# Attention that feeds a routed expert layer: where v is issued, where exp of q stands, and how the first weights are issued

## The chip, the cores and the metric

The kernel runs on one core of one Trainium2 chip. The metric is the device time of one execution in microseconds (us). Before the change it is 229.13 us, the median of three runs (229.08, 229.13, 229.18).

## The reference

There are two stages. The first is an attention without a score matrix; q, k and v have 8 batches, 8 heads, 576 positions and 64 features per head. The second sends each of the 4608 resulting rows of 512 numbers to one of 8 experts, chosen by a hash of its token id.

```python
def _attn_ref(q, k, v):
    q_s = np.exp(q - np.max(q, axis=-1, keepdims=True))
    q_s = q_s / (np.sum(q_s, axis=-1, keepdims=True) + 1e-09)
    k_s = np.exp(k - np.max(k, axis=2, keepdims=True))
    k_s = k_s / (np.sum(k_s, axis=2, keepdims=True) + 1e-09)
    kv = np.einsum('bhsd,bhse->bhde', k_s, v)
    return np.einsum('bhsd,bhde->bhse', q_s, kv)

def _moe_ref(x, token_ids, w1, w2):          # x: 4608 rows of 512
    expert_idx = token_ids * np.int64(2654435761) % np.int64(8)
    for e in range(8):
        mask = expert_idx == e
        out[mask] = np.maximum(x[mask] @ w1[e], 0.0) @ w2[e]
    return out
```

## The kernel before

**Order.** Every engine gets one stream of instructions, in the order in which the Python code emits them. `em.op` and `em.dma` add an instruction to a stream together with the semaphore waits that its buffers need (`R` read, `W` written, `P` written in part). An instruction that waits holds up everything behind it in its own stream. So the order of the calls in the loop over batches is, engine by engine, the order of the work.

**Loads.** `load(b, p)` lets SyncE issue q and k of batch b (L291) into one of two buffers each; q of batch b+2 can be issued when exp of q of batch b is done, k of batch b+2 when exp of k of batch b is done. `load_v(b, n)` lets GpSimd issue v (L304), with a conversion to bf16 on the way, into slot n of four. The expert weights are issued by GpSimd too: `weights1_half` (L668), `weights1` (L660), `weights2` (L674). The first expert's weights lie where q and k of the even batches were.

**One batch, b, with p = b % 2.** In the order of the calls:

- `exp_k(p)`: ScalarE takes exp of k (L518) into `ek`.
- `transpose_q(p)`: TensorE transposes `eq` (L525); VectorE and ScalarE copy the result to `qT` (L535, L537, L538).
- `one_hot(b)`: VectorE builds the matrices that put rows in the order of their experts (L592).
- `sort(1-p, 0, 3)`: TensorE sorts the first two of four column blocks of batch b-1 by expert (L601), ScalarE copies the result to `xs` (L608, two instructions); this copy is called an evacuation. `sort(1-p, 2, 0)`, the second one, does the other two blocks. It stands behind `kv` except in the last batch, where it stands ahead of it.
- `kv(p, n)`: TensorE multiplies exp of k with v (L550; "the matmul with v"), VectorE divides by the sums (L555, L559).
- `exp_q(1-p, 0)` and `exp_q(1-p, 1)`: ScalarE takes exp of q of batch b+1 (L514), in two instructions.
- `qsum(p)` and `attend(p, ...)`: TensorE (L569, L577), and VectorE scales the rows into `xn` (L573, L582).
- `segments(b-1)`: GpSimd copies 16 segments of `xs` of batch b-1, eight experts by two groups of rows, to their places in `xT` (L645). `segments` is a generator; each `next` emits one copy. `run(gen, n)` emits up to n copies, all 16 by default. The addresses come from registers that `load_segments` loads. In the last two batches a part of the copies is done by VectorE.

The v of batch b+2 is issued in batch b ahead of these copies for b = 1 to 4 (v2 already in batch 0); v7 is issued in batch 6. In batch 6 the first expert's first weights follow it (two halves by columns, each in two parts, four issues of L668), and the copies of batch 5 stand behind them.

**The expert stage.** When the last batch is sorted, TensorE runs both layers for eight experts in turn: `l1` (L683) with its rectifier on ScalarE or VectorE (L690, L692), then `layer2` (L708). GpSimd scatters the rows to the output (L724). The first two steps of `l1` are emitted ahead of the last batch's sort. Columns 0 to 511 of the first layer's weights wait for the first half of the weights, columns 512 to 1023 for the second.

Of the kernel before, what the change touches and what calls it, by code (L numbers as in the profile page):

```python
# [164 lines left out]
def fused_kernel(nc, q, k, v, moe_token_ids, moe_w1, moe_w2, out):  # L165
    B, H, S, DH = q.shape
    NTOK = moe_token_ids.shape[0]
    E, D, F = moe_w1.shape
# [109 lines left out]
    def dv(fn, R=(), W=(), P=()):  # L278
        em.op("dve", fn, R, W, P)

    def ac(fn, R=(), W=(), P=()):
        em.op("act", fn, R, W, P)
# [5 lines left out]
    b_q, b_k = [Buf(), Buf()], [Buf(), Buf()]  # L288

    def load_one(nm, dst, src, b, p, bb):  # L290
        em.dma("sync", nm % p, lambda e: e.dma_start(  # L291
            dst[p][:].rearrange("p h c d -> p h (c d)"),
            src[b].rearrange("(a h) (p c) d -> (h p) a (c d)", h=2, p=64)), W=[bb[p]])
# [8 lines left out]
    def load_v(b, n, R=()):  # L302
        o = 3 * (n % 2)
        em.dma("pool", "d_v%d" % n, lambda e: e.dma_start(  # L304
            vx[n // 2][:, o:o + 2, :, :, :].rearrange("p a j c d -> p (a j) (c d)"),
            v[b].rearrange("(a h) (p c) d -> (h p) a (c d)", h=2, p=64)), R=R, W=[b_vx[n]])
# [24 lines left out]
    for h in range(2):  # L331
        for a in range(2):
# [8 lines left out]
       R=[b_tok], P=[b_ei])  # L341
# [9 lines left out]
       R=[b_ef2, bc["iota8"]], W=[b_flg])  # L351
# [5 lines left out]
          R=[b_flg, bc["upper"], bc["ones"]], W=[bk[6], bk[7]])  # L357
# [13 lines left out]
       R=[b_pr], W=[b_pos])  # L371
# [137 lines left out]
    def load(b, p):  # L509
        load_one("d_q%d", qf, q, b, p, b_q)  # L510
        load_one("d_k%d", kf, k, b, p, b_k)

    def exp_q(p, j):
        ac(lambda e: e.activation(eq[p][:, j, :, :, :].rearrange("p c a d -> p a c d"),  # L514
                                  qf[p][:, j::2, :, :], ACTF.Exp), R=[b_q[p]], W=[b_eq[p][j]])

    def exp_k(p):
        ac(lambda e: e.activation(ek[p][:].rearrange("p j c a d -> p a (j c) d"),  # L518
                                  kf[p][:].rearrange("p (a j) c d -> p a (j c) d", a=2), ACTF.Exp),
           R=[b_k[p]], W=[b_ek[p]])  # L520
# [21 lines left out]
    def kv(p, n):  # L542
        o, one = (0, 2) if n % 2 == 0 else (2, 0)
        a0 = 1 - one // 2
        fns = []
        for j in range(2):
            for c in range(NC):
                for h2 in range(2):
                    r = slice(64 * h2, 64 * h2 + 64)
                    fns.append(lambda e, j=j, c=c, h2=h2, r=r: e.matmul(  # L550
                        PB[:, 6 + h2, 192 * j:192 * j + 192], ek[p][r, j, c, :, :].rearrange("p a d -> p (a d)"),
                        vx[n // 2][r, o:o + 3, j, c, :], start=(c == 0), stop=(c == NC - 1)))
        em.op("pe", fns, R=[b_ek[p], b_vx[n]], W=[bk[6], bk[7]])
        KV = PB[:, 6:8, 0:384].rearrange("p h (j a x) -> p j h a x", j=2, a=3)
        dv(lambda e: e.reciprocal(out=rk[p][:].rearrange("p (j h) -> p j h", h=2), in_=KV[:, :, :, one, 0]),  # L555
           R=[bk[6], bk[7]], W=[b_rk[p]])
        for a in range(2):
            r = slice(64 * a, 64 * a + 64)
            dv(lambda e, a=a, r=r: e.tensor_tensor(  # L559
                out=kvn[p][r, :, a, :].rearrange("p (j h) x -> p j h x", h=2), in0=KV[r, :, :, a0 + a, :],  # L560
                in1=rk[p][r, :].rearrange("p (j h) -> p j h", h=2).unsqueeze(3).to_broadcast([64, 2, 2, DH]),
                op=ALU.mult), R=[bk[6], bk[7], b_rk[p]], W=([b_kvn[p]] if a == 0 else ()),
               P=(() if a == 0 else [b_kvn[p]]))
# [24 lines left out]
    def one_hot(b):  # L588
        p = b % 2
        for t in range(T):  # L590
            g, i = t // TG, t % TG
            dv(lambda e, g=g, i=i: e.tensor_scalar(  # L592
                out=oneh[p][g][:, i, :], in0=col16[:, 0:GW[g]], scalar1=pos[:, 2 * b + g, i:i + 1],
                scalar2=None, op0=ALU.is_equal),
               R=[b_pos, bc["col16"]], W=([b_oh[p][g]] if i == 0 else ()), P=(() if i == 0 else [b_oh[p][g]]))
# [23 lines left out]
    def load_segments(b, key, half=None):  # L619

        def ld(e):
            k = (key, half, b % 2 if half is not None else 0)
            if k not in regs:
                regs[k] = [e.alloc_register("rg%s%d_%d" % (key, i, len(regs)))
                           for i in range(4 * E if half is None else 2 * E)]
            rs = regs[k]
            if half is None:
                e.load(rs, rgi[0:1, 2 * b:2 * b + 2, :].rearrange("p g x -> p (g x)"))
            else:
                for g in range(2):  # L630
                    e.load(rs[8 * g:8 * g + 8], rgi[0:1, 2 * b + g, 8 * half:8 * half + 8])
        em.raw(key, ld, R=[b_rg])

    def segments(b, key="pool", half=None):
        p = b % 2
        for g in range(2):
            for ee in range(E) if half is None else range(4 * half, 4 * half + 4):
                def seg(e, ee=ee, g=g):
                    if half is None:
                        rs, o = regs[key, None, 0], 2 * E * g + 8 * (ee // 4) + ee % 4  # L640
                    else:
                        rs, o = regs[key, half, p], 8 * g + ee % 4
                    so = e.snap(rs[o], min_val=0, max_val=GW[g])  # L643
                    do = e.snap(rs[o + 4], min_val=CAPS * ee, max_val=CAPS * ee + CAP)
                    return e.tensor_copy(out=xT[:, :, bass.ds(do, SEG[g])],  # L645
                                         in_=xs[p][:, :, XO[g]:XO[g] + GW[g] + SEG[g]][:, :, bass.ds(so, SEG[g])])
                em.op(key, seg, R=b_xs[p] + ([] if b < B - 2 else [b_x5[ee]]), W=[(b_x5 if b < B - 2 else b_x7)[ee]])
                yield
# [16 lines left out]
    def weights1_half(ee, s, hf, R=()):  # L665
        fs = slice(hf * F // 2, hf * F // 2 + F // 2)
        for a in range(2):
            em.dma("pool", "d_w1h%d" % hf, lambda e, a=a: e.dma_start(  # L668
                w1b[s][64 * a:64 * a + 64, :, fs], moe_w1[ee].rearrange("(a g p) f -> a p g f", a=2, g=4)[a, :, :, fs]), R=R,
                W=([b_w1[s][hf]] if a == 0 else ()), P=(() if a == 0 else [b_w1[s][hf]]))  # L670
# [59 lines left out]
    def run(gen, n=2 * E):  # L730
        for _ in range(n):
            if next(gen, 0) == 0:
                break
# [7 lines left out]
    for b in range(B):  # L741
        p = b % 2
        last = b == B - 1
        exp_k(p)
        transpose_q(p)
        one_hot(b)
        if b > 0:
            sort(1 - p, 0, 3)
        if last:
            sort(1 - p, 2, 0)  # L750
        if b + 2 < B:
            load(b + 2, p)
        kv(p, b % 4)
        if 0 < b < B - 1:
            sort(1 - p, 2, 0)
        if not last:
            exp_q(1 - p, 0)
            exp_q(1 - p, 1)
        qsum(p)
        if b == 0:  # L760
            load_v(2, 2)
        elif b < B - 3:
            load_v(b + 2, (b + 2) % 4)
        elif b == B - 2:
            load_v(B - 1, 3)
        if b == B - 2:
            for s, bs in enumerate(([b_q[0], b_k[0]], [b_q[1], b_k[1]])):
                b_w1[s], b_w2[s] = [Buf(*bs), Buf(*bs)], Buf(*bs)
            weights1_half(0, 0, 0)
            weights1_half(0, 0, 1)  # L770
            load_segments(b - 1, "pool")
            run(segments(b - 1))
        elif last:
            weights1(1, 1)
            weights2(0, 0)
            for x in (b - 1, b):
                load_segments(x, "pool", 1)
                load_segments(x, "dve", 0)
            run(segments(b - 1, "pool", 1))
        elif b > 0:  # L780
            load_segments(b - 1, "pool")
            run(segments(b - 1))
        attend(p, 0, 2, 3)
        attend(p, 2, 2, 6)
        attend(p, 4, 1, 5)
        if b == 0:
            segment_table()
            widths()
        if b == 1:
            overflow()  # L790
        if b == 2:
            load_widths()
# [121 lines left out]
    for b in range(B):  # L914
# [11 lines left out]
        for ch in range(4):  # L926
# [4 lines left out]
                R=b_xn[0] + [b_id], W=bk[u:u + 2])  # L931
            ac(lambda e, ch=ch, u=u: e.activation(xg[:, ch, :].rearrange("p (h x) -> p h x", h=2),
                                                  PB[:, u:u + 2, 0:H2], ACTF.Copy), R=bk[u:u + 2], W=[b_xg[ch]])
        for ee in range(E):
# [5 lines left out]
            for t in range(T):  # L940
                u = layer2(NW, t, 2)
                m = flg[:, 2 * b + t // TG, ee, t % TG:t % TG + 1]
                if ee == 0:
                    dv(lambda e, t=t, u=u, m=m: e.tensor_scalar(out=yg[:, t, :], in0=PB[:, u, :], scalar1=m,
                                                                scalar2=None, op0=ALU.mult),
                       R=[bk[u], b_flg], W=[b_yg[t]])
                else:
                    dv(lambda e, t=t, u=u, m=m: e.scalar_tensor_tensor(
                        out=yg[:, t, :], in0=PB[:, u, :], scalar=m, in1=yg[:, t, :], op0=ALU.mult, op1=ALU.add),
                       R=[bk[u], b_flg], W=[b_yg[t]])  # L950
# [39 lines left out]
```

## Time and profile before

| | |
|---|---|
| median of three runs | 229.13 us |
| the profiled execution: its time, its span | 230.2 us, 228.4 us |
| busy: TensorE, VectorE, ScalarE, GpSimd | 198.9, 116.1, 105.7, 121.6 us |
| mean granted TensorE clock | 0.992 |
| exp of k (L518) starts, batch 1 to 7 | 20.19, 31.44, 40.53, 51.23, 60.87, 69.01, 77.15 us |
| v issued by GpSimd (L304), batch 2 to 7 | 12.9, 28.47, 36.35, 43.42, 52.53, 73.16 us |
| last k: issued, landed | 63.07, 73.7 us |
| unbroken run of TensorE in the expert stage | from 91.91 us |

The span runs from the first to the last instruction of the profiled execution; all starts count from its beginning. The four lines on batches come from the timelines of the engines and from the DMA answers (issue and time to landing). The idle time in front of a group of instructions stands in square brackets, with what ended it.

### The profile page before, as it was taken

What the parts mean: (1) busy time and instruction counts of PE and PEld (TensorE: products, weight loads), DVE (VectorE), ACT (ScalarE), POOL (GpSimd) and SP (SyncE); (2) the same over time, 40 slices, a digit from 0 to 9 for tenths busy, and PEclk for the clock granted to TensorE, in tenths of its full rate; (3) what the DMA queues carried; (4) which work ended last, traced back from release to release, by engine and by line L of the source; (5) the groups of instructions that cost most, each with busy time, mean ns of one, the idle gap of its engine ahead of it and who ended that gap; (6) DMA issues with size and microseconds to landing.
All of it is one profiled execution on the core that took longest, in us unless ns stands there. A gap on an engine that the chain in (4) does not pass through costs nothing.

```text
span 228.4 us, 4640 instructions
## 1 busy us (share of the span) xinstructions
PE 198.9 (87%) x1786; PEld 134.5 (59%) x1788; DVE 116.1 (51%) x265; ACT 105.7 (46%) x133; POOL 121.6 (53%) x235
## 2 busy tenths in 40 slices
PE   0459968876899788999999999999999999999990
PEld 0348757654776564775574764754855845845640
DVE  1678798782778867699941322322421422412220
ACT  3385588756888944765342331331422322322311
POOL 8740778773659993670007975805715615125053
PEclk9999999997999999999999999999999999999999
DMA  6999999999996999799993799999999798113023
GB/s 208 295 371 293 292 372 316 301 312 351 297 401 250 149 196 195 119 153 204 207 177 139 160 204 205 330 272 201 290 200 242 163 203 224 73 46 139 24 102 123
DMA packets 29776, 50.25 MB, mean 220 GB/s; under 512 B 2351, under 2 KB 15663, under 8 KB 29744
## 3 DMA queue, kind: packets, MB, share of 16 engines
q0 software_dynamic: 20768, 30.94, 67.1%
q1 hardware_dynamic: 8976, 18.91, 22.9%
q8 instruction: 16, 0.26, 0.4%
q14 instruction: 16, 0.13, 0.2%
HBM read 61.90 MB, written 10.49 MB: 317 GB/s over the span
## 4 chain that ended last, share of the span: by engine, by line
PE 62%; DMA 20%; POOL 6%; ACT 5%; issue 4%; POOLq 1%; DVE 1%; SPq 1%; DVEq 0%; ACTq 0%
PE ps L708 29%; PE ps L683 27%; DMA kf<-in_k_dram 20%; POOL xT L645 4%; PE ps L601 3%; ACT ek L518 3%; PE ps L550 2%; ACT eq L514 1%; POOL out_dram L724 1%; ACT xs L608 1%; PE ps L819 1%; DVE xn L582 1%; POOLq L643 1%; POOL w1b L668 0%; POOL w1b L660 0%
## 5 line engine op out<-in xcount | busy, mean ns | idle before, releaser
L724 POOL DMA_INDIRECT out_dram<-yo,idx x40 | 39.5, 987 | 71.6 <-ACT yo L718 31.8
L708 PE MATMUL ps<-w2b,hT 128*128 128x512 bf16 x320 | 70.4, 379 | 0.0
L683 PE MATMUL ps<-xT,w1b 128*128 128x320 bf16 (+1 forms) x512 | 64.4, 286 | 0.8 <-ACT hT L690 0.8
L683 PEld LDWEIGHTS ps<-xT,w1b 128*128 128x128 bf16 x512 | 49.7, 98 | 15.1 <-ACT hT L690 1.1
L708 PEld LDWEIGHTS ps<-w2b,hT 128*128 128x128 bf16 x320 | 31.2, 98 | 36.3
L645 POOL COPY xT<-xs x112 | 39.6, 412 | 19.4 <-ACT xs L608 17.9
L690 ACT ACTIVATE hT<-ps 128x640 bf16<-128x640 f32 x41 | 28.8, 703 | 39.4 <-PE ps L683 39.0
L718 ACT ACTIVATE yo<-ps 128x512 f32<-128x512 f32 x26 | 15.5, 597 | 54.1 <-PE ps L708 54.1
L692 DVE TENSOR_SCALAR hT<-ps 128x640 bf16<-128x640 f32 x23 | 19.0, 825 | 30.2 <-PE ps L683 30.2
L720 DVE COPY yo<-ps 128x512 f32<-128x512 f32 x14 | 9.7, 692 | 44.0 <-PE ps L708 44.0
L601 PE MATMUL ps<-oneh,xn 128*128 128x384 bf16 (+1 forms) x160 | 25.0, 307 | 1.3 <-ACT qT L537 1.0
L582 DVE TENSOR_TENSOR xn<-ps,rq 128x1024 bf16<-128x1024 f32 (+1 forms) x24 | 23.6, 1041 | 3.2 <-PE ps L577 2.6
L608 ACT ACTIVATE xs<-ps 128x768 bf16<-128x768 f32 (+1 forms) x32 | 19.1, 651 | 9.2 <-PE ps L601 9.1
L518 ACT ACTIVATE ek<-kf 128x2304 bf16<-128x2304 f32 x8 | 17.0, 2123 | 9.9 <-DMA kf<-in_k_dram 9.9
L550 PE MATMUL ps<-vx,ek 64*128 64x192 bf16 x288 | 15.2, 264 | 7.2 <-ACT ek L518 7.2
L601 PEld LDWEIGHTS ps<-oneh,xn 128*128 128x128 bf16 x160 | 14.8, 102 | 10.1 <-issue 2.5
L514 ACT ACTIVATE eq<-qf 128x1152 bf16<-128x1152 f32 x16 | 17.7, 1162 | 2.0 <-DMA qf<-in_q_dram 2.0
L550 PEld LDWEIGHTS ps<-vx,ek 64*128 64x128 bf16 x288 | 12.9, 102 | 9.0 <-ACT ek L518 8.5
L525 PE MATMUL ps<-ident,eq 128*128 128x128 bf16 x144 | 12.2, 244 | 5.0 <-ACT eq L514 5.0
L525 PEld LDWEIGHTS ps<-ident,eq 128*128 128x128 bf16 x144 | 10.0, 111 | 6.1 <-ACT eq L514 5.7
L592 DVE TENSOR_SCALAR oneh<-col,pos 128x384 bf16<-128x384 f16 (+1 forms) x40 | 13.5, 403 | 0.0
L674 POOL DMA_DIRECT2D w2b<-in_moe_w_dram x16 | 12.4, 798 | 0.0
(101 smaller groups left out, 131.1 us busy)
## 6 DMA issues: line engine op xcount, KB each, us to landing
qf<-in_q_dram SPq DMA_DIRECT2D x8, 1152.0 KB, 15.7
kf<-in_k_dram SPq DMA_DIRECT2D x8, 1152.0 KB, 16.9
w2b<-in_moe_w_dram POOLq DMA_DIRECT2D x16, 512.0 KB, 11.5
w1b<-in_moe_w_dram POOLq DMA_DIRECT2D x14, 512.0 KB, 9.3
vx<-in_v_dram POOLq DMA_DIRECT2D x8, 576.0 KB, 11.1
w1b<-in_moe_w_dram POOLq DMA_DIRECT2D x4, 256.0 KB, 7.8
out_dram<-yo,idx POOLq DMA_INDIRECT x40, 4.4
tok<-in_moe_token_ids_dram SPq DMA_DIRECT2D x1, 36.0 KB, 5.6
```

The source lines that it names most:

```text
L514: ac(lambda e: e.activation(eq[p][:, j, :, :, :].rearrange("p c a d -> p a c d"), qf[p][:, j::2, :, :], ACTF.Exp), R=[b_q[p]], W=[b_eq[p][j]])
L518: ac(lambda e: e.activation(ek[p][:].rearrange("p j c a d -> p a (j c) d"), kf[p][:].rearrange("p (a j) c d -> p a (j c) d", a=2), ACTF.Ex ...
L525: return e.transpose(PBH[:, o:o + 128], eq[p][:, j, c, :, :].rearrange("p a d -> p (a d)"), ident[:])
L550: fns.append(lambda e, j=j, c=c, h2=h2, r=r: e.matmul(PB[:, 6 + h2, 192 * j:192 * j + 192], ek[p][r, j, c, :, :].rearrange("p a d -> p (a ...
L582: dv(lambda e: e.tensor_tensor(out=xn[p][:, t0:t0 + n, :].rearrange("p t (g x) -> p (t g) x", x=DH), in0=PB[:, bank:bank + n, :].rearrange ...
L601: em.op("pe", [lambda e, g=g, i=i, k=k, n=n: e.matmul(PB[:, bank + (k if g == 0 else 2), (0 if g == 0 else GW[1] * k):(GW[0] if g == 0 els ...
L608: ac(lambda e, g=g, src=src: e.activation(xs[p][:, c0:c0 + 2, XO[g]:XO[g] + GW[g]], src, ACTF.Copy), R=bs, P=b_xs[p][c0:c0 + 2])
L645: return e.tensor_copy(out=xT[:, :, bass.ds(do, SEG[g])], in_=xs[p][:, :, XO[g]:XO[g] + GW[g] + SEG[g]][:, :, bass.ds(so, SEG[g])])
L683: em.op("pe", [lambda e, d=d, k=k: e.matmul(cut(PB[:, u + k, 0:H2]), w1b[s][:, d, 128 * (f + k):128 * (f + k) + 128], cut(rhs(d)), start=( ...
L690: ac(lambda e: e.activation(o, i, ACTF.Relu), R=bk[u:u + 2], W=[b_hT[hp][hf][f // 2]])
L708: em.op("pe", [lambda e, fc=fc: e.matmul(PB[:, u, :], hT[hp][:, fc, 128 * t:128 * t + 128], w2b[s][:, fc, :], start=(fc == 0), stop=(fc == ...
L724: em.dma("pool", "d_o%d" % y, lambda e: e.indirect_dma_start(out=out[:, :], out_offset=IndirectOffsetOnAxis(ap=idx[:, 5 * ee + t:5 * ee + ...
```

## The change

Three things are moved, and nothing is added to the computation. First, in batches 0 to 6 the two exp instructions of the next q stand ahead of `kv` and of the second sort, so ScalarE does them before the second evacuation. Second, v2 is issued once k1 has landed; v4, v5, v6 and v7 are issued in batches 2, 3, 4 and 5, each behind the first of the 16 segment copies of that batch (v3 stays in batch 1, ahead of them). Third, in batch 6 the first half of the first weights is issued behind the first segment copy and the second half behind seven more, where both halves stood ahead of all the copies.

```diff
         if b + 2 < B:
             load(b + 2, p)
+        if not last:
+            exp_q(1 - p, 0)
+            exp_q(1 - p, 1)
         kv(p, b % 4)
         if 0 < b < B - 1:
             sort(1 - p, 2, 0)
-        if not last:
-            exp_q(1 - p, 0)
-            exp_q(1 - p, 1)
         qsum(p)
         if b == 0:
-            load_v(2, 2)
-        elif b < B - 3:
-            load_v(b + 2, (b + 2) % 4)
-        elif b == B - 2:
-            load_v(B - 1, 3)
+            load_v(2, 2, R=[b_k[1]])
+        elif b == 1:
+            load_v(3, 3)
         if b == B - 2:
             for s, bs in enumerate(([b_q[0], b_k[0]], [b_q[1], b_k[1]])):
                 b_w1[s], b_w2[s] = [Buf(*bs), Buf(*bs)], Buf(*bs)
+            load_segments(b - 1, "pool")
+            sg = segments(b - 1)
+            run(sg, 1)
             weights1_half(0, 0, 0)
+            run(sg, E - 1)
             weights1_half(0, 0, 1)
-            load_segments(b - 1, "pool")
-            run(segments(b - 1))
+            run(sg)
...
         elif b > 0:
             load_segments(b - 1, "pool")
-            run(segments(b - 1))
+            sg = segments(b - 1)
+            run(sg, 1)
+            if 1 < b < B - 2:
+                load_v(b + 2, (b + 2) % 4)
+            run(sg)
```

## The prediction

> **What bounds the kernel now.** I read the chain of waits first: from 92 us on it is TensorE alone (L683 and L708 in turn, no idle), so the expert stage ends a fixed time after the last batch's sort. In front of that, the timeline of ScalarE shows when each batch b may start: exp of k (L518, "ek b" below), then seven more instructions in order.
>
> ```profile
> 51.23 2.12 ACT L518 ACTIVATE ek<-kf 128x2304 bf16<-128x2304 f32 x1 [2.45 <-DMA kf<-in_k_dram]
> ...
> 57.69 1.19 ACT L608 ACTIVATE xs<-ps 128x768 bf16<-128x768 f32 x2 [2.35 <-PE ps L601]
> ...
> 60.87 2.12 ACT L518 ACTIVATE ek<-kf 128x2304 bf16<-128x2304 f32 x1
> ...
> 73.97 1.19 ACT L608 ACTIVATE xs<-ps 128x768 bf16<-128x768 f32 x2 [0.84 <-PE ps L601]
> 75.04 2.22 ACT L514 ACTIVATE eq<-qf 128x1152 bf16<-128x1152 f32 x2
> 77.15 2.12 ACT L518 ACTIVATE ek<-kf 128x2304 bf16<-128x2304 f32 x1
> ```
>
> ek 4 at 51.23 waited for k4. After that ScalarE runs through: ek 5, 6, 7 start at 60.87, 69.01, 77.15, that is 8.14 us apart, with 0.84 us idle in each batch ahead of the second evacuation (L608). From ek 7 to the first matmul of the unbroken run (91.91) are 14.8 us that the change leaves in their order. So the time moves as ek 7 moves.
>
> The second view is the table of stretches (columns: PE, PEld, DVE, ACT, POOL busy, clock, DMA share, GB/s), the third the DMA answers for 58 to 60 us and for k7 and v7.
>
> ```profile
> 54.00:58.00 4.00, 4.00 (x39) 2.64 (x36) 1.03 (x3) 1.65 (x4) 0.00 (x0) 0.57 1.06 362
> 58.00:59.00 1.00, 1.00 (x33) 1.00 (x31) 0.39 (x1) 1.00 (x3) 0.00 (x0) 1.00 1.12 290
> 65.00:66.00 1.00, 1.00 (x11) 0.74 (x10) 0.81 (x2) 0.17 (x1) 0.00 (x0) 1.00 1.08 421
> 72.00:73.00 1.00, 1.00 (x24) 0.78 (x19) 0.51 (x3) 1.00 (x3) 1.00 (x5) 1.00 0.42 155
> ```
>
> ```profile
> q0 software_dynamic: 171, 0.20, 56.6%
> q1 hardware_dynamic: 171, 0.38, 55.3%
> ...
> vx<-in_v_dram POOLq DMA_DIRECT2D x1, 576.0 KB, 6.0
> ...
> kf<-in_k_dram SPq DMA_DIRECT2D x1, 1152.0 KB, 10.6
> ```
>
> The DMA engines are full from 3 to 72 us. q and k go in order through the hardware queue, v through the software queue. Alone, the first moves about 409 GB/s (64 to 66 us); beside a v it falls to 0.38 MB in 2 us, 190 GB/s, while v gets 98. A q or k (1.18 MB) is 2.88 us alone. A v (0.59 MB) flows for 6.0 us and costs the other queue 6.0 x (409-190)/409 = 3.2 us. k7, issued at 63.07, lands at 73.7, and v7 is issued only then:
>
> ```profile
> 52.53 0.74 POOL L304 DMA_DIRECT2D vx<-in_v_dram  x1
> 59.13 5.67 POOL L645 COPY xT<-xs  x16 [5.86 <-ACT xs L608]
> 67.56 5.66 POOL L645 COPY xT<-xs  x16 [2.75 <-ACT xs L608]
> 73.16 0.74 POOL L304 DMA_DIRECT2D vx<-in_v_dram  x1
> ```
>
> Last, TensorE: after 2.54 us without work its clock fell to 0.50 for 3.4 us (54.2 to 57.6), and ten matmuls of the sort took 2.55 instead of 1.47 us. At 79.3 it idled 0.98 us and stayed at 1.00.
>
> ```profile
> 53.40 2.21 PE L550 MATMUL ps<-vx,ek 64*128 64x192 bf16 x36 [2.54 <-ACT ek L518]
> 55.55 2.55 PE L601 MATMUL ps<-oneh,xn 128*128 128x384 bf16 x10
> ...
> 77.88 1.47 PE L601 MATMUL ps<-oneh,xn 128*128 128x384 bf16 x10
> 80.33 1.47 PE L601 MATMUL ps<-oneh,xn 128*128 128x384 bf16 x10 [0.98 <-ACT qT L537]
> ```
>
> **exp of q moved.** Two L514 (2.2 us together) go ahead of two L608; nothing is added. TensorE's transposes no longer wait for them (0.39 + 0.43 us a batch in the late ones). But the gain is not that: sort, matmul with k, second sort, attend, VectorE's scaling and the next sort follow one another, by the rows of batch 5 1.59 + 1.32 + 0.50 + 0.69 + 2.35 (two of three scalings) + 0.05 + 1.44 = 7.94 us against 8.14. So 0.2 us a batch where nothing is awaited. The price: the second evacuation, and the copies and v behind it on GpSimd, come up to 2.2 us later, and with them exp waits for q to land. SP issues each q about 2 us sooner, which changes no order in a queue that is never empty.
>
> **v2 waits for k1.** k1 lands at 20.19; v2's issue moves from 12.9 to 20.2. Behind it on GpSimd is L381, idle until 23.65 anyway: nothing. v1 flows until about 22.3, so v2 flows 24.3 to 30.3 and lands at 32.0, and the matmul needs it at 33.6: nothing, with 1.6 us in hand. v3 keeps its 28.47.
>
> **v4 to v7 behind a copy.** Issue = end of the second evacuation + 0.25 (as 58.88 to 59.13) + 0.35 for one copy. The bytes begin 4.05 us after the issue (28.47 to 32.5; 52.53 to 56.5), flow 6.0 us and are landed 1.75 us later (38.5 to 40.3). For q and k I run the two rates on from k3, whose bytes are through at 38.7 by the running sum of the queue; done for the kernel before, this gives ends that the landings follow by 2.1 us (alone) or 3.3 us (beside a v), and k7 at 71.4, landed 73.7. exp of q starts when q has landed, and 4.1 us behind ek at the earliest (60.87 to 64.99); the evacuation ends 1.1 us behind it, or 3.9 us behind the start of the matmul with v. Now the change, batch by batch.
>
> v4 is issued at 39.6 (evacuation after q3's exp, 35.6 to 37.8, ends at 39.0), flows 43.7 to 49.7, lands 51.4. q4 is through at 41.6, landed 43.7; k4: 2.1 us alone, then 0.32/0.19 = 1.7, through 45.4, landed 48.7, which is 2.5 us sooner than before. ek 4 at 48.7, but its matmul waits for v4: 51.4 (before 53.4).
>
> v5: exp of q4 44.6 to 46.8, evacuation to 47.9, issue 48.5, flows 52.6 to 58.6, lands 60.3. q5 through 50.6, landed 52.7; k5 54.6, landed 57.9. The matmul of batch 5 waits for v5: 60.3 (before 63.05).
>
> v6: exp of q5 52.9 to 55.1, evacuation to 56.2, issue 56.9, flows 60.9 to 66.9, lands 68.6. q6 through 59.6, landed 61.7; k6 64.4, landed 67.7. Matmul of batch 6 at 67.7 + 2.2 = 69.9 (before 71.19).
>
> v7: exp of q6 62.1 to 64.3, evacuation to 65.4, issue 66.0, bytes from 70.1. q7 is through at 68.6. k7: 1.5 us alone (0.61 MB), the rest beside v7, 0.57/0.19 = 3.0 us, through 73.1, landed 76.4. So v7 gives k7 a delay of 2.7 us, which the slack of 77.15-73.7 = 3.4 us nearly takes up.
>
> ScalarE would be free for ek 7 at 75.1 (exp of q7 71.8 to 74.0, then the evacuation). It waits for k7: 76.4. **The sum**: 76.4-77.15 = -0.75 us; span 228.4 to 227.65, profiled 230.2 to 229.45. The profiled time is 1.07 above the median, so the median goes to 229.13-0.75 = 228.4. The bounds of this term: v7 issued 1 us sooner puts k7 at 77.5 (+0.35), 1 us later at 75.2 (-1.95).
>
> Against this the page "DMA: Bandwidth & Descriptors" of the Trainium skill, section "Rules for kernel authors", says to issue a DMA early and wait late; its section "Anatomy of one DMA" gives 2.0 us plus bytes at 436 GB/s, by estimate 3.4 us for a v, whose 0.59 MB would delay k7 by 1.4 us, to 75.1, and the time would be 227.1. The trace has 11.3 us for v6 beside q and k, and I keep the row.
>
> **First weights in two issues.** The same four L668 (2.48 us) now stand behind one and behind eight copies. The evacuation ends at 75.1 as before (75.16), so the first half is issued at 75.8 and 76.4 instead of 73.9 and 74.5; with the 7.3 us that its second part took before it lands at 83.7, needed by the first L683 at 85.70-0.75 = 85.0. The second half, issued at 79.5 and 80.2, lands 8.9 us later at 89.1, needed at 91.2. Expert 1's weights follow when the copies are through, at 75.4 + 5.65 + 2.5 = 83.6 instead of 81.92; with 8.4 us (81.92 to the second landing, 90.3) they land at 92.0, needed two steps of 1.05 us behind 91.2, at 93.3. All are covered by 1.3 us; uncovered, they would cost what they are late. The copies themselves start up to 2.5 us sooner; nobody on the path waits for them.
>
> **The rivals.** (1) Slower: TensorE cools. While ek 7 waits for k7, the sort of batch 6 ends at 77.8 (69.9 + 7.94) and the next sort waits for the qT copy, 3.0 us behind ek 7, at 79.4: 1.6 us idle, against 0.98 now. The clock held at gaps of 1.05 us and fell at 2.54; between lies the point from which this decides. If it falls, 3.4 us at half speed hit that sort and the matmul with v: batch 0's matmul with v, cold, took 3.06 us for 1.66, the sort above 2.55 for 1.47. Half of 3.4 us, 1.7, is the most that is lost; with 1.6 the time is 230.0, slower than before. The page "TensorE: Matmul & The Clock Gate", Part 1, names an idle window of about 3.4 us; by that 1.6 us would cost nothing and the sum would stand; but the 2.54 us above did cost.
> (2) Faster: v7's bytes begin at 71 or later (a later matmul of batch 5), pass behind k7, and ScalarE sets ek 7 at 75.1 to 75.3: -1.95, 227.2.
> (3) v7 flows wholly ahead of k7's end: 73.7 + 3.2 = 76.9 up to 77.5, so 228.9 to 229.5, and the rest of the change brings nothing.
>
> **How the numbers follow.** Forecast 0.47, own range 227.6 to 229.2; rival 1 0.27; rival 2 0.14; rival 3 0.12. A run of this kernel can tell about 0.2%, 0.46 us. Faster by more (ek 7 before 76.7): 0.31 of the forecast's share and all of rival 2, 0.45. Within: 0.14 of the forecast and half of rival 3, 0.20. Slower: rival 1, the other half of rival 3 and 0.02 of the forecast, 0.35. The range takes in rival 2's end and rival 1 with 0.6 more: 227.2 to 230.6.
>
> **What would show it.** ek 4 near 48.7 with its matmul held until about 51.4, matmul of batch 5 near 60.3, no half clock at 54; v7 issued near 66; ek 7 idle ahead of it on kf, near 76.4. Wrong if ek 7 starts without waiting for k7, if the clock drops after 78 us, or if the first L683 waits for w1.

## The result, and the profile after

The changed kernel takes 229.25 us (median of 4 runs, 228.99 to 229.48), the kernel before 229.16 in the same comparison. The ratio is 1.0004 with a 95% interval of 0.9987 to 1.0021: no change that can be told. Measured again in a second comparison, it is 0.9997 (0.9980 to 1.0015). Ratios go by fast runs; the only slow one below, a run of e3 at 231.37 us, is left out of its ratio.

The profiles say something else at first sight: the span went from 228.4 to 227.2 us. The timeline of ScalarE in the changed kernel, with the idle time ahead of a group in brackets:

```profile
47.63 2.15 ACT L518 ACTIVATE ek<-kf 128x2304 bf16<-128x2304 f32 x1
...
58.10 2.12 ACT L518 ACTIVATE ek<-kf 128x2304 bf16<-128x2304 f32 x1 [1.86 <-DMA kf<-in_k_dram]
...
67.69 2.12 ACT L518 ACTIVATE ek<-kf 128x2304 bf16<-128x2304 f32 x1 [2.29 <-DMA kf<-in_k_dram]
...
73.79 1.20 ACT L608 ACTIVATE xs<-ps 128x768 bf16<-128x768 f32 x2
75.86 2.12 ACT L518 ACTIVATE ek<-kf 128x2304 bf16<-128x2304 f32 x1 [0.86 <-DMA kf<-in_k_dram]
```

Batch 4 starts 3.6 us sooner than the 51.23 of before. But batches 5, 6 and 7 now each wait for their k, which before they did not, and of the 3.6 us 1.29 are left at batch 7 (75.86 for 77.15). The unbroken run of TensorE starts at 90.62, 14.76 us behind, as before. GpSimd's timeline and the DMA answers show what the last k shares its way with:

```profile
65.95 0.46 POOL L645 COPY xT<-xs  x1 [2.96 <-ACT xs L608]
66.46 0.74 POOL L304 DMA_DIRECT2D vx<-in_v_dram  x1
```

```profile
vx<-in_v_dram POOLq DMA_DIRECT2D x1, 576.0 KB, 9.9
...
kf<-in_k_dram SPq DMA_DIRECT2D x1, 1152.0 KB, 15.5
```

v7, issued at 66.46, lands at 76.4; k7, issued at 60.29, lands at 75.8, where it landed at 73.7 before. In the table of stretches (PE, PEld, DVE, ACT, POOL busy, clock, DMA share, GB/s) the changed kernel has no half clock at 54 us; it has one from about 39.6 to 43 us. Its DMA engines are still full at 72 us, with v7 beside k7 (264 GB/s), when before they had largely run dry (0.42, 155 GB/s):

```profile
39.00:40.00 1.00, 0.46 (x5) 0.59 (x8) 1.00 (x2) 0.87 (x2) 0.00 (x0) 0.80 1.05 417
40.00:41.00 1.00, 1.00 (x13) 1.00 (x11) 1.00 (x3) 0.54 (x1) 0.81 (x2) 0.50 1.04 408
...
54.00:58.00 4.00, 3.96 (x68) 3.43 (x66) 3.04 (x6) 1.98 (x3) 2.00 (x5) 1.00 1.13 288
...
72.00:73.00 1.00, 1.00 (x17) 0.81 (x16) 0.63 (x2) 1.00 (x2) 0.46 (x2) 1.00 1.16 264
```

So there were two questions. Why do 1.2 us of span not appear in the time? And is v7 what holds the last k?

### The profile page after: what moved, and what is told of

Same layout as the page of the kernel before. It is cut to its first block, busy times and chain, and to the rows that moved or that the text cites. A ratio compares the mean times of both kernels' runs of the same rounds, so it can differ in the third digit from the quotient of the medians.

```text
span 227.2 us, 4641 instructions
## 1 busy us (share of the span) xinstructions
PE 197.4 (87%) x1786; PEld 134.2 (59%) x1788; DVE 122.4 (54%) x265; ACT 105.6 (46%) x133; POOL 122.2 (54%) x235
## 4 chain that ended last, share of the span: by engine, by line
PE 60%; DMA 24%; ACT 4%; issue 4%; DVE 3%; POOL 2%; DVEq 1%; SPq 1%; POOLq 0%; ACTq 0%
PE ps L708 28%; PE ps L683 27%; DMA kf<-in_k_dram 19%; DMA vx<-in_v_dram 5%; PE ps L601 3%; ACT ek L518 2%; POOL out_dram L724 2%; DVE xn L582 2%; PE ps L550 1%; DVEq L631 1%; ACT eq L514 1%; ACT qT L537 1%; SPq L291 1%; PE ps L824 1%; ACT xs L608 0%
## 5 line engine op out<-in xcount | busy, mean ns | idle before, releaser
L724 POOL DMA_INDIRECT out_dram<-yo,idx x40 | 39.6, 990 | 71.5 <-ACT yo L718 31.8
L683 PEld LDWEIGHTS ps<-xT,w1b 128*128 128x128 bf16 x512 | 49.8, 98 | 14.9 <-ACT hT L690 1.1
L518 ACT ACTIVATE ek<-kf 128x2304 bf16<-128x2304 f32 x8 | 17.0, 2127 | 13.4 <-DMA kf<-in_k_dram 13.4
L592 DVE TENSOR_SCALAR oneh<-col,pos 128x384 bf16<-128x384 f16 (+1 forms) x40 | 19.6, 556 | 0.0
L550 PE MATMUL ps<-vx,ek 64*128 64x192 bf16 x288 | 13.6, 246 | 6.6 <-ACT ek L518 5.0
L550 PEld LDWEIGHTS ps<-vx,ek 64*128 64x128 bf16 x288 | 11.7, 95 | 8.2 <-ACT ek L518 6.2
L577 PE MATMUL ps<-kvn,qT 128*128 128x128 bf16 x160 | 11.3, 231 | 2.1 <-DVE kvn L559 2.1
```

Source lines behind the costliest of these rows:

```text
L550: fns.append(lambda e, j=j, c=c, h2=h2, r=r: e.matmul(PB[:, 6 + h2, 192 * j:192 * j + 192], ek[p][r, j, c, :, :].rearrange("p a d -> p (a ...
L592: dv(lambda e, g=g, i=i: e.tensor_scalar(out=oneh[p][g][:, i, :], in0=col16[:, 0:GW[g]], scalar1=pos[:, 2 * b + g, i:i + 1], scalar2=None, ...
L683: em.op("pe", [lambda e, d=d, k=k: e.matmul(cut(PB[:, u + k, 0:H2]), w1b[s][:, d, 128 * (f + k):128 * (f + k) + 128], cut(rhs(d)), start=( ...
L724: em.dma("pool", "d_o%d" % y, lambda e: e.indirect_dma_start(out=out[:, :], out_offset=IndirectOffsetOnAxis(ap=idx[:, 5 * ee + t:5 * ee + ...
```

## The experiments

Theory A: the profiled execution of before was one of its longer ones, lengthened by the half clock at 54 us. Theory C: the toll is v7, whose bytes flow ahead of the last k. Their rivals (B, D, E and others) stand in the expectations. "Last exp of k" is the start of L518 of batch 7. Medians are of 9 to 12 runs (e12: one run); ratios are to the kernel before, run beside them.

| run | what it is | median us | ratio (95%) | last exp of k | last k landed |
|---|---|---|---|---|---|
| e1_before_again | before | 229.92 | 1.0003 (0.9980 to 1.0026) | 77.43 | 73.65 |
| e12_before_third | before, one run | 229.13 | - | 76.04 | 73.8 |
| e8_warm | before, gap filled | 229.46 | 0.9996 (0.9975 to 1.0016) | 75.92 | 73.7 |
| e2_after_again | changed | 229.47 | 0.9997 (0.9980 to 1.0015) | 75.85 | 75.8 |
| e3_expq_only | exp of q alone | 228.30 | 0.9937 (0.9914 to 0.9959) | 74.81 | 73.4 |
| e4_without_expq | changed, exp of q back | 229.66 | 1.0001 (0.9984 to 1.0019) | 76.54 | 76.5 |
| e5_k3_free | changed, k3 not held | 229.60 | 1.0005 (0.9984 to 1.0027) | 76.11 | 76.1 |
| e6_v7_late | changed, v7 late | 228.06 | 0.9928 (0.9903 to 0.9952) | 74.38 | 73.3 |
| e7_expq_v7 | exp of q, v7 early | 228.75 | 0.9987 (0.9952 to 1.0022) | 75.35 | 75.3 |
| e9_expq_weights | exp of q, weights | 228.16 | 0.9942 (0.9923 to 0.9962) | 75.03 | 73.7 |
| e10_v7_late_v2_early | e6, v2 at once | 228.31 | 0.9940 (0.9917 to 0.9963) | 75.10 | 73.8 |
| e11_v6_ahead | e10, v6 ahead of the copies | 228.44 | 0.9955 (0.9929 to 0.9982) | 75.07 | 73.7 |

**Which execution of before the profile showed.** e1_before_again and e12_before_third are the kernel before, unedited; e2_after_again is the changed one.

> The kernel before, unchanged, for a second profile and its spread. Theory A: the profiled execution shown so far was 1.07 us above its median because of the half clock at 54 to 58 us, which most executions don't have. Then a new profile has a span near 227.3 us, no half clock behind 50 us, batch 5's exp of k near 59.8 and the last one near 76.1 us instead of 77.15. Rival B: the half clock is regular; then the span is 228.4 again with the last exp of k at 77.15, and the 1.3 us that the change gained there in its profile are lost in its other executions.

> The changed kernel, unchanged, for a second profile. Theory A: span 227.1 to 227.7 us, last exp of k at 75.8 to 76.4 us behind a wait for the last k, expert stage as before (136.6 us from the unbroken run to the end); time as before within 0.2%. Rival B: the last exp of k again near 75.9 us, but a half clock behind 78 us or a longer stage behind it, 228.4 us of span.

> The kernel before, unchanged, one more profile. Theory A: of its executions some have the half clock at 54 us (near 230.5 us) and more have not (near 229.2 us). If this one lies below 229.8 us, it has no half clock between 50 and 58 us and its last exp of k starts near 75.9 to 76.3 us; if it lies above 230 us, it has it, and the last exp of k starts near 77.2. Rival: the two don't go together.

e1's profiled execution took 230.62 us and had the half clock again, from 53.6 to 57 us. Theory A had expected a profile without it, so after e1 rival B stood. Its other runs lie from 229.07 to 230.54. One more profile, e12, caught an execution of 229.13 us. Its stretches and ScalarE's timeline:

```profile
38.00:42.00 4.00, 2.51 (x32) 2.60 (x35) 3.66 (x6) 3.09 (x3) 4.00 (x11) 0.78 1.09 339
42.00:46.00 4.00, 4.00 (x55) 3.13 (x52) 2.58 (x8) 2.98 (x4) 2.24 (x7) 0.79 1.12 289
54.00:58.00 4.00, 4.00 (x80) 3.45 (x74) 1.81 (x5) 3.16 (x6) 1.39 (x4) 1.00 1.04 406
```

```profile
72.85 1.19 ACT L608 ACTIVATE xs<-ps 128x768 bf16<-128x768 f32 x2 [0.84 <-PE ps L601]
73.93 2.22 ACT L514 ACTIVATE eq<-qf 128x1152 bf16<-128x1152 f32 x2
76.04 2.12 ACT L518 ACTIVATE ek<-kf 128x2304 bf16<-128x2304 f32 x1
```

Here the half clock lies a batch earlier, from about 40 to 44 us, ahead of the wait for k4, which takes the loss up; TensorE then comes late to that wait and idles 0.80 us there instead of 2.54. The clock stays full at 54, and the last exp of k starts at 76.04. Three profiles of before thus go with theory A: 230.2 and 230.62 us with the drop at 54, 229.13 us without. e2 for its part repeats the changed kernel's profile: 75.85, behind a wait for k7, with the runs from 228.95 to 230.03.

**Filling the gap.** In the kernel before, with `warm()` new:

```diff
+        if b == 4:
+            warm()     # 28 matmuls of ident with ones into bank 6, which kv overwrites
         kv(p, b % 4)
```

> The kernel before with 28 matmuls of 128 columns on constants (about 1.8 us) in front of batch 4's matmul with v, in the gap in which TensorE waits for k4; their result is overwritten. Theory A (the kernel before has executions with a half clock at 54 us and executions without, about 1.2 us apart): no half clock near 54 us, batch 5's exp of k near 60 us, the last one near 76.0 to 76.3, no time above 229.8 us, median 229.1 to 229.4. Rival: the half clock is not what parts the executions; then times near 230.5 us remain, or the last exp of k stays at 77.2.

No run of 12 lies above 229.94 us, where 10 of the 34 runs of before beside it lie above 230.0. Batch 5 starts at 59.28 and the last exp of k at 75.92. So the upper times go with the half clock at 54 us: they are gone when TensorE has work in the gap. Two expectations were missed: two runs lie just above 229.8 us (229.82 and 229.94), and the median, 229.46, is not lower than that of before (229.42), against the 229.1 to 229.4 expected. Only the upper part of the spread went.

**One part of the change at a time.** e3 is the kernel before with only the exp moved; e4 is the changed kernel with only that move taken back:

```diff
 e3 (against before)                     e4 (against the changed kernel): the reverse
+        if not last:
+            exp_q(1 - p, 0)
+            exp_q(1 - p, 1)
         kv(p, b % 4)
         if 0 < b < B - 1:
             sort(1 - p, 2, 0)
-        if not last:
-            exp_q(1 - p, 0)
-            exp_q(1 - p, 1)
```

> Only exp of q moved; v and the weights as in the kernel before. Theory A: with v early and v7 late the last k lands near 73.7 us, so ScalarE and TensorE set the last exp of k: 0.2 us a batch over the last three, 0.6 us, near 75.5 us, time 0.5 to 0.7 us below before. Rival: the move gains nothing, because exp of q now waits for q to land in batches 1 to 4 and the second evacuation comes late; then the time is that of before within 0.2 us.

> The change without the move of exp of q: v and the first weights as changed, exp of q behind the second sort as before. Theory A: the last k lands near 76 to 77 us because v7 flows ahead of it, and the last exp of k waits for it: time 0 to 0.8 us above before. Rival: v costs nothing there, ScalarE's own order sets the last exp of k at 8.14 us a batch from an earlier batch 4; then the time is up to 1 us below before.

The move of exp of q alone is worth 0.63% (0.41% to 0.86%); the medians are 1.25 us apart (229.55 and 228.30), about twice the 0.5 to 0.7 us expected. In its profile k7 has landed at 73.4 and ScalarE comes to the last exp of k from its own work:

```profile
73.75 1.20 ACT L608 ACTIVATE xs<-ps 128x768 bf16<-128x768 f32 x2
74.81 2.15 ACT L518 ACTIVATE ek<-kf 128x2304 bf16<-128x2304 f32 x1
```

Without it the v's and the weights change nothing that can be told (1.0001), and the last exp of k stands at 76.54 behind k7. So the whole change is a gain of 0.6% that its other part takes back, though by itself that part costs nothing that can be told.

**Is it v7?** e6 is the changed kernel with v7 in batch 6 again; e7 is e3 with v7 alone in batch 5:

```diff
 e6, batches 2 to 5 and batch 6
-            if 1 < b < B - 2:
+            if 1 < b < B - 3:
                 load_v(b + 2, (b + 2) % 4)
...
+            load_v(B - 1, 3)
             load_segments(b - 1, "pool")
             sg = segments(b - 1)
 e7, against e3: the load_v(B - 1, 3) of batch 6 gone, and
-            run(segments(b - 1))
+            sg = segments(b - 1)
+            run(sg, 1)
+            if b == B - 3:
+                load_v(B - 1, 3)
+            run(sg)
```

> The changed kernel with v7 issued in batch 6 again, ahead of the copies; all else as changed. Theory C: the last k lands near 73.0 to 73.7 us, the last exp of k is set by ScalarE near 74.8 to 75.1, time 0.8 to 1.1 us below the changed kernel, about that of the kernel in which only exp of q moved. Rival D: the last exp of k stays at 75.5 or later and the time within 0.3 us of the changed kernel.

> Exp of q moved, and of the v's only v7, into batch 5 behind the first copy; v2 to v6 and the weights as in the kernel before. Theory C: this alone gives the toll: the last k lands 2 to 2.7 us later than with v7 late (73.42), near 75.5 to 76, the last exp of k waits for it, time 0.8 to 1.2 us above the kernel in which only exp of q moved. Rival D: the last exp of k stays near 74.8 and so does the time.

With v7 late (issued at 72.0) k7, issued at 60.23, lands at 73.3 instead of 75.8, and the last exp of k follows ScalarE's own work:

```profile
kf<-in_k_dram SPq DMA_DIRECT2D x1, 1152.0 KB, 13.1
```

```profile
73.30 1.19 ACT L608 ACTIVATE xs<-ps 128x768 bf16<-128x768 f32 x2 [0.62 <-PE ps L601]
74.38 2.12 ACT L518 ACTIVATE ek<-kf 128x2304 bf16<-128x2304 f32 x1
```

The kernel is 0.72% (0.48% to 0.97%) faster than before. Here the last exp of k no longer sets the expert stage. TensorE's own rows do, with both sorts of batch 6 in one piece:

```profile
70.52 1.66 PE L550 MATMUL ps<-vx,ek 64*128 64x192 bf16 x36 [0.84 <-DMA vx<-in_v_dram]
...
77.03 2.78 PE L601 MATMUL ps<-oneh,xn 128*128 128x384 bf16 x20 [0.82 <-DVE xn L582]
...
89.94 5.32 PE L683 MATMUL ps<-xT,w1b 128*128 128x320 bf16 x38
```

The sort waits for VectorE's scaling behind batch 6's matmul with v, which had waited for v6, and the unbroken run starts 15.56 us behind the last exp of k instead of 14.76. So the 0.43 us that this exp starts ahead of e3's (74.38 for 74.81) are not passed on: e3's unbroken run starts at 89.65.

e7 is the counter-test: v7 alone, issued at 67.7, lets k7 (issued at 61.11) land at 75.3, where it landed at 73.4 in e3:

```profile
kf<-in_k_dram SPq DMA_DIRECT2D x1, 1152.0 KB, 14.2
```

The last exp of k starts 0.54 us behind that of e3, less than the 0.8 to 1.2 us that the time was expected to rise. Only about 0.25 us of it are the wait for k7: ScalarE was free at 75.10 (1.06 us behind the start of the evacuation at 74.04, as in e3). The other 0.29 us were there in batch 6 (67.94 for 67.65), when v7 had only just been issued. v7 was also issued 1.2 us later than in the changed kernel, so e7 shows the delay of the last k, 1.9 us, but little of its price. Its ratio is too wide to say more: 3 of the 12 runs lie from 230.6 to 231.6 us, as does one of e3's ten (231.37), and what lengthened them stays open.

**A wait that I had missed.** The changed kernel's SyncE timeline:

```profile
18.24 0.37 SPq L291 DMA_DIRECT2D qf<-in_q_dram  x1
32.09 0.37 SPq L291 DMA_DIRECT2D kf<-in_k_dram  x1
```

k3 is issued at 32.09, not at 22.4. `load_v(2, 2, R=[b_k[1]])` makes v2 wait for k1, as meant, but it also enters v2 as a reader of k1's buffer, so the load of k3 into that buffer waits until v2 has landed (20.94 + 11.1 = 32.04), and q4 queues behind it. e5 keeps the first wait and drops the second:

```diff
-            load_v(2, 2, R=[b_k[1]])
+            em.raw("pool", lambda e: None, R=[b_k[1]])
+            load_v(2, 2)
```

> The changed kernel, but GpSimd's wait for k1 in front of v2 no longer makes v2 a reader of k1's buffer, so k3 is issued when exp of k1 is done (near 22.8 us instead of 32, when v2 has landed). Theory C (the toll is v7, which flows ahead of the last k): the last k lands near 75.8 us as in the changed kernel, the time moves by less than 0.3 us. Rival D (the toll is the late k3, which leaves the queue of q and k short of work from 33 to 36 us, 253 instead of 290 GB/s): every later k lands 0.3 to 1.0 us sooner, the last exp of k near 75.2, and the time is that much below the changed kernel.

k3 is issued at 22.92 and lands at 40.62, where it landed at 40.4; the last k lands at 76.1 and the time does not move. Rival D falls. In the changed kernel the queue of q and k did run short from 34 to 36 us (0.15 MB, 0.38 before), but v3 moved 0.33 MB in that time instead of 0.19, and from 38 to 40 us k3 had the engines to itself (0.82 MB).

**Weights, v2, v6.** e9 is e3 with the weights' two issues; e10 is e6 with a plain `load_v(2, 2)`; e11 is e10 with v6 ahead of the copies of batch 4.

> Exp of q moved and the first weights in two issues between the copies; all v as in the kernel before. Theory C: the weights are covered, so the last exp of k stays near 74.8, the first L683 behind it by 8.6 us as ever, the time within 0.3 us of the kernel in which only exp of q moved (ratio to before 0.9937). Rival E: the weights, issued 2 us later, hold up the first L683 or the copies shift the last sort; then the unbroken run starts later than 14.8 us behind the last exp of k and the time rises by as much.

> The changed kernel with v7 issued in batch 6 ahead of the copies and v2 issued at once as in the kernel before. Theory C: v2 plays no part; last exp of k near 74.4 to 75.0, time within 0.3 us of the kernel with v7 late alone (ratio to before 0.9928). Rival D: v2's wait costs or saves something; then the time moves by 0.4 us or more.

> As the one before it (v7 in batch 6, v2 at once), and v6 issued ahead of the copies of batch 4 as in the kernel before; v4 and v5 behind the first copy. With v7 late the matmul of batch 6 waited for v6 (70.39 us). Theory C: v6 lands 2 to 4 us sooner, k6 up to 1.5 us later (near 67.5), batch 6's matmul starts near 69.7, the last exp of k near 74.0 to 74.4, time 0 to 0.5 us below the kernel with v7 late. Rival: k6 takes the place of v6 and the last exp of k stays at 74.4 to 75.0.

e9 and e10 came out as theory C said: neither the weights nor v2 can be seen in the time, and in e9 the unbroken run starts 14.9 us behind the last exp of k. e11 did not. v6 landed at 66.7 and k6 at 67.8, but TensorE's clock had fallen:

```profile
66.98 1.93 PE L525 MATMUL ps<-ident,eq 128*128 128x128 bf16 x18 [1.58 <-ACT xs L608]
68.70 2.42 PE L601 MATMUL ps<-oneh,xn 128*128 128x384 bf16 x10
71.05 1.66 PE L550 MATMUL ps<-vx,ek 64*128 64x192 bf16 x36
```

Behind 1.58 us without work the transposes took 1.93 us instead of 1.17 and the sort 2.42 instead of 1.47, so batch 6's matmul with v started at 71.05, not 69.7, and the last exp of k at 75.07. As in e6, that matmul sets the expert stage: the unbroken run starts 15.40 us behind the last exp of k and, as in e6, 19.42 us behind the matmul. The run says nothing on v6 itself. e3, e6, e9, e10 and e11 are 0.45 to 0.72% faster than the kernel before, whose time the changed kernel has; their intervals overlap, so none can be called the best.

## Why the prediction was right or wrong

The measured time lies in the range, but the forecast of -0.75 us did not come: the ratio says none. The forecast's own range, 227.6 to 229.2 us, was missed too, by 0.05 us. That the whole range holds the time is owed to its width, which takes in rivals on both sides; no change that can be told had been given 0.20. The steps, one by one.

**Right: the path.** In the changed kernel the time moves as the last exp of k moves, and that waits for the last k. (In e6 and e11 the matmul with v of batch 6 takes over, as shown above.) Forecast: batch 4's matmul with v held by v4 to 51.4, batch 5's by v5 at 60.3, batch 6's at 69.9, v7 issued at 66.0, k7 landed 76.4. Measured: 52.27 and 60.49, both released by v, 69.87, 66.46, 75.8. The toll of v7 was put at 2.7 us; e6 shows 2.5 (75.8 - 73.3). TensorE idled 1.18 us ahead of the last second sort, not 1.6, and in this profile its clock held, so rival 1 did not come.

**Wrong: what the -0.75 was taken from.** The step that failed reads "The profiled time is 1.07 above the median, so the median goes to 229.13-0.75". The 1.07 was carried along as if it lay outside the sum. It lay inside: 77.15 was the last exp of k of an execution with the half clock at 54 us, and the profiled execution near the median, 229.13 us, has it at 76.04 (e12; e8, with the gap filled, at 75.92). Against that the forecast 76.4 would have been +0.4, and the measured 75.86 is -0.18 us, 0.1%, which is no change that can be told. The row with 0.57 in the clock column stood in the prediction; it was used for rival 1 and not for the kernel before itself.

**Wrong: a point between 1.05 and 2.54 us from which the clock falls.** No such point on the length of a gap shows in the runs. The changed kernel's clock fell at 39.6 us behind gaps of 0.92 and 0.89 us, and e11's behind 1.58; it held behind 1.50 us in e5, ahead of the very sort that rival 1 names, and behind 2.09 us in e7. So that rival 1 stayed away does not show its condition to be right.

**Wrong: "queue that is never empty".** SP was said to issue each q about 2 us sooner. It issued k3 9.7 us and q4 1.9 us later, because the added `R` holds up the load of k3 as well as v2, and from 34 to 36 us the queue of q and k ran short. e5 shows that this cost nothing that can be told.

**Half right: the worth of the parts.** "0.2 us a batch where nothing is awaited" for exp of q was too small as a whole: alone it brings 1.23 us in the last exp of k (76.04 to 74.81). In e3's profile batch 4 starts at 49.78 instead of 51.35 (e12): the later evacuation also puts v5 and v6 off (issued at 45.4 and 55.7 instead of 43.5 and 54.4), and k4 lands 1.5 us sooner. That the one makes the other was not tried by itself, so the source of the gain stays open. The step from batch 6 to 7 is 7.16 us there, less than the chain of 7.94 that I had as its floor: that chain bounds TensorE, and the exp of k may run ahead of it. Its size was right: up to the start of the sort it was put at 6.50 us, and from batch 6's matmul with v to that start it takes 6.51 in the changed kernel, e3, e6 and e11 alike. Rival 3 names the time that came (228.9 to 229.5), but not how: k7 landed at 75.8, not at 76.9 or later.

Against the page "DMA: Bandwidth & Descriptors" of the Trainium skill, whose section "Rules for kernel authors" says to issue a DMA early: with v7 issued 5.5 us later (72.0 for 66.46) the kernel takes 0.72% less than the kernel before, where the changed one takes the same. Here the DMA engines are full, and the early v7 takes its share from k7, which is needed first.

## What to carry to other kernels

Where the DMA engines are full, a load that is brought forward can be paid for by the load that lands last in front of a waiting engine; ask for each transfer which one it will share its way with, and issue it when that one is through. Before a sum is made on a profiled execution, ask what makes it differ from the median: an effect that comes and goes must be taken out of the start of the sum. When a wait is added through a dependency tracker, look up what else it enters: a wait for a buffer can make the waiting transfer a reader that the next load of the buffer waits for.

## What the runs showed of the hardware

The place of TensorE's half clock differs from execution to execution of one kernel: in the kernel before it fell at 54 us for 3.4 us in two profiles and at about 40 us in the third, (0.22 + 0.21) x 4 / 0.5 = 3.4 us again. The page "TensorE: Matmul & The Clock Gate" of the Trainium skill, Part 1, says that the activity window of about 3.4 us runs freely and does not start with the kernel, which fits. It puts the drop behind an idle window of that length; here 2.54 us without work, with busy time before and behind, were enough, in e11 1.58 us, in e12 two gaps of 1.30 and 0.86 us, and in the changed kernel two of 0.92 and 0.89 us. In e7 the clock held at 1.00 behind a longer gap:

```profile
58.70 1.18 PE L525 MATMUL ps<-ident,eq 128*128 128x128 bf16 x18 [2.09 <-ACT xs L608]
```

So the length of one gap does not decide, and no run here shows what does. A drop costs only where it meets the path: at 54 us it cost about 1.1 us (77.15 - 76.04), and at 40 us in e12 a wait for k4 took it up. The changed kernel's two profiles say the same: one has a drop at 39.6 us, the other (e2) none between 23 and 95 us, and the last exp of k starts at 75.86 and 75.85.
